# One unit's front split by heads, squares taken in pairs, five transposes moved to DMA

## The chip, the cores and the metric

The kernel runs on one core of one Trainium2 chip. The metric is the device time of one execution in microseconds (us). The profile records one execution and gives its span.

Engine names are those of the profile: PE does the matrix products, PEld its weight loads, DVE is the vector engine, ACT the scalar engine, POOL is GpSimd, and SP shows nothing but issues of DMA in these profiles. "SPq" and "POOLq" mean the issuing of DMA by those engines. Every program here has two DMA queues that matter: q1, fed by SP (`hardware_dynamic` on the page, 72528 packets before), and q0, fed by POOL (`software_dynamic`, 1088 packets).

A run is called fast or slow by comparing its time with the fastest run of the same kernel in the same batch, so a batch in which every run is long is called fast throughout. I therefore also say "short" for runs below 186 us and "long" for runs above 186 us when I speak of the kernel before, whose 47 later runs have nothing between 184.62 and 186.91.

## The reference

A gated linear recurrence over 768 positions, with 4 batches, 8 heads and head size 48, feeds a dense block with squared relu.

```python
def _attn_ref(q, k, v, alpha):
    state = np.zeros((B, H, D, D), dtype=np.float32)
    for t in range(S):
        state = alpha[:, :, t, :, None] * state + np.einsum('bhd,bhe->bhde', k[:, :, t], v[:, :, t])
        y[:, :, t] = np.einsum('bhd,bhde->bhe', q[:, :, t], state)
    return y

def _moe_ref(x, w_in, w_out):          # x: 3072 x 384, w_in: 384 x 2048, w_out: 2048 x 384
    h = x @ w_in
    r = np.maximum(h, 0.0)
    return (r * r) @ w_out
```

## The kernel before

The work is cut into 12 units of 256 tokens (4 batches, 3 stages). Each unit has a *front* (cumulative decay from alpha, scaled k and q, their transposes), the attention products, a transpose of the attention output `xbf` into `xt`, and the dense block: `s1` (w_in), relu, square, `s2` (w_out).

The program is a list of operations. A scheduler written in Python plays it through with estimated costs, and what comes out is a **fixed order of instructions for each engine**. In the traces each engine takes its list in that order and waits on semaphores. So a late input stops what stands behind it in the same list: in the long profile of after ACT was idle for 9.20 us before the cast of a late v (37.91 us), and the four instructions behind it in the list started after it (38.66 to 39.76 us).

The parts that the argument touches:

```python
# all of them move by DMA; order of the loads is steered by "after"
def weight(lay, w):
    cut = slice(w * FS * 128, (w + 1) * FS * 128) if lay == 0 else slice(w * FS, (w + 1) * FS)
    if lay == 0:
        src, dst = moe_w_in.rearrange("(kk p) n -> p kk n", p=128)[:, :, cut], WIN[:, :, cut]
    else:
        src = moe_w_out[w * FS * 128:(w + 1) * FS * 128, :].rearrange("(p e) n -> p (e n)", e=FS)
        dst = WOUT[:, cut, :].rearrange("p e n -> p (e n)")
    key = ("win", "wout")[lay]
    load_op[key, w] = add("pool", lambda e: e.dma_start(dst, src), ...,          # queue q0
                          after=[load_op[AFTER[key, w]]] if (key, w) in AFTER else [])

def load(g):                                                                     # queue q1
    for j, t, nm in ((0, alpha, "a"), (1, k, "k"), (2, q, "q"), (3, v, "v")):
        src = t[b, :, t0:t0 + T, :].rearrange("h (p j) d -> p h (j d)", j=2)     # pieces of 384 bytes
        ...
AFTER = {("win", 0): (1, "a"), ("win", 1): (1, "a"), 2: ("win", 0), ("wout", 0): (2, "a"),
         ("wout", 1): (2, "a"), 3: ("wout", 0)}

# the attention output of a unit, transposed by PE
def xtr(pe):
    for c in range(2):
        for kk in range(KT):
            o = c * KT + kk
            ins = pe.matmul(to[:, c, kk], src[:, o * 128:(o + 1) * 128], IDENT[:], is_transpose=True)
    return ins
add("pe", xtr, ..., reads=[("xbf", x2), ("ident",)], writes=[("ps", "X", 0)])
add("dve", lambda e: e.tensor_copy(dst, bank[:, 0:KT * T]), ..., writes=[("xt", s)])   # or ACT

# relu and square, 512 elements at a time
add("act", lambda e, hb=hb, rb=rb: e.activation(RR[rb][:], psH[hb], AF.Relu), ...)     # or DVE
add("dve", lambda e, dst=dst, sq=sq: e.tensor_tensor(dst, sq, sq, ALU.mult), 415, ...) # or POOL or ACT
# ... (cut)
pr.schedule()
pr.fill(...)       # dummy matmuls ("fillers") in PE's early gaps
pr.place()         # semaphore waits
pr.emit()
```

In words, the start is a chain of loads. Alpha of the second unit lands, then w_in is issued. w_in lands, then alpha, k, q, v of the third unit are issued on q1. When alpha of the third unit lands, w_out is issued on q0. When w_out lands, the loads of the fourth unit are issued. I count units from one; the chain view and the code count them from zero.

## Time and profile before

| | value |
|---|---|
| three timed runs | 191.17, 191.76, 192.35 us |
| the profiled execution | span 180.1 us, time 181.86 us, granted PE clock 1.00 |
| PE, DVE, ACT busy | 174.7, 130.6, 118.6 us |

The profile's page of the kernel before, in part. The second line is busy time with its share of the span and the number of instructions; the row of digits is PE's busy tenths in 40 slices of the span; the queue lines give packets, megabytes and share of the 16 DMA engines.

```profile
span 180.1 us, 5336 instructions
...
PE 174.7 (97%) x2333; PEld 138.7 (77%) x2333; DVE 130.6 (73%) x228; ACT 118.6 (66%) x220; POOL 17.7 (10%) x25
...
PE   7998999999999999999999999999999999999994
...
q1 hardware_dynamic: 72528, 28.32, 65.3%
q0 software_dynamic: 1088, 3.15, 9.2%
```

PE is busy in nearly every slice. q0 carries 1088 packets for 3.15 MB, q1 carries 72528 packets for 28.32 MB: the packets of q0 are large, those of q1 small.

PE's list of waits in the same kernel (engine, line, what it waited for: us in total, times, longest):

```profile
PE psO L896 <- DVE zero L417: 1.3, 1, 1.3
PE psWH L822 <- DMA win<-in_moe_w_in_dram: 0.7, 1, 0.7
PE psWH L541 <- ACT lab L535: 0.4, 1, 0.4
```

The third line: the cumulative-sum product of the third unit waits 0.4 us for an ACT result.

The chain of waits of the same kernel (start us, us, what), only its long DMA pieces:

```profile
4.23 4.86 DMA raw<-in_alpha_dram
...
9.38 8.61 DMA win<-in_moe_w_in_dram
...
18.00 5.32 DMA raw<-in_alpha_dram
...
23.61 8.45 DMA wout<-in_moe_w_out_dram
...
35.72 5.47 DMA raw<-in_v_dram
```

One load releases the next up to about 41 us; after that the chain is nearly all PE work. Two groups of instructions that the change touches (line, engine, operation, count, busy us, mean ns, then idle time before them):

```profile
L836 DVE TENSOR_TENSOR gt<-rr 128x512 bf16<-128x512 bf16 x61 | 26.5, 438 | 19.8 <-ACT rr L830 19.4
...
L774 PE MATMUL psX<-ident,xbf 128*128 128x128 bf16 x72 | 6.0, 219 | 0.1
```

### The profile page before, as it was taken

To read this page: it belongs to the slowest core of one execution; us is meant where nothing else is said; L and a number is where in the kernel's file an instruction comes from. 1 tells how busy PE (TensorE), PEld (TensorE's weight loads), DVE (VectorE), ACT (ScalarE), POOL (GpSimd) and SP (SyncE) were. 2 spreads that over 40 slices of the span, in tenths; PEclk is the share of its full clock that TensorE was granted. 3 is DMA by queue.
4 is the path that set the end of the run, shared out by engine and by line. 5 is a ranking of instruction groups with operands and counts; after the bars stand their busy time and mean duration, and the time that the engine had idled before them with its cause. 6 is when DMAs were issued, how large, how long until landed. Compare 5 with 4: busy or idle time off the path is not lost.

```text
span 180.1 us, 5336 instructions
## 1 busy us (share of the span) xinstructions
PE 174.7 (97%) x2333; PEld 138.7 (77%) x2333; DVE 130.6 (73%) x228; ACT 118.6 (66%) x220; POOL 17.7 (10%) x25
## 2 busy tenths in 40 slices
PE   7998999999999999999999999999999999999994
PEld 5786887866787688877688778787788787788773
DVE  6499577898977988969998888789649655534130
ACT  4762788677786887858677758567557554656451
POOL 3030020323020010242002101000000000000000
DMA  5999999999999998999999994713512510110112
GB/s 147 323 290 192 253 249 207 222 264 284 210 279 235 302 254 221 250 260 279 271 188 306 274 266 136 153 56 60 107 44 34 130 47 0 47 44 0 47 44 87
DMA packets 73639, 31.80 MB, mean 177 GB/s; under 512 B 69392, under 2 KB 72592, under 8 KB 73616
## 3 DMA queue, kind: packets, MB, share of 16 engines
q1 hardware_dynamic: 72528, 28.32, 65.3%
q0 software_dynamic: 1088, 3.15, 9.2%
q8 instruction: 18, 0.29, 0.7%
q14 instruction: 5, 0.04, 0.1%
HBM read 25.17 MB, written 4.72 MB: 166 GB/s over the span
## 4 chain that ended last, share of the span: by engine, by line
PE 74%; DMA 18%; SPq 4%; DVE 2%; issue 1%; ACT 1%
PE psO L853 30%; PE psWH L822 30%; DMA raw<-in_alpha_dram 6%; DMA win<-in_moe_w_in_dram 5%; DMA wout<-in_moe_w_out_dram 5%; SPq L495 4%; DMA raw<-in_v_dram 3%; PE psX L678 3%; PE psX L671 2%; PE psX L732 2%; PE psZ L651 2%; PE psX L774 2%; PE psX L795 1%; PE psZ L732 1%; PE psWH L541 1%
## 5 line engine op out<-in xcount | busy, mean ns | idle before, releaser
L822 PE MATMUL psWH<-xt,win 128*128 128x256 bf16 x576 | 73.3, 274 | 0.9 <-DMA win<-in_moe_w_in_dram 0.7
L822 PEld LDWEIGHTS psWH<-xt,win 128*128 128x128 bf16 x576 | 64.9, 145 | 5.6 <-DVE kqt L622 1.0
L853 PE MATMUL psO<-wout,gt 128*128 128x384 bf16 x368 | 68.9, 326 | 0.1
L830 ACT ACTIVATE rr<-psWH 128x512 bf16<-128x512 f32 x80 | 47.1, 595 | 22.5 <-PE psWH L822 21.2
L853 PEld LDWEIGHTS psO<-wout,gt 128*128 128x128 bf16 x368 | 34.5, 98 | 18.7 <-DMA wout<-in_moe_w_out_dram 0.4
L836 DVE TENSOR_TENSOR gt<-rr 128x512 bf16<-128x512 bf16 x61 | 26.5, 438 | 19.8 <-ACT rr L830 19.4
L839 ACT ACTIVATE gt<-rr 128x512 bf16<-128x512 bf16 x35 | 21.5, 626 | 1.6 <-DVE rr L832 1.2
L860 ACT ACTIVATE osb<-psO 128x384 f32<-128x384 f32 x22 | 10.8, 490 | 13.9 <-PE psO L853 13.6
L741 DVE TENSOR_TENSOR pm<-psX,caus 128x1024 bf16<-128x1024 f32 x12 | 14.7, 1221 | 4.0 <-PE psZ L732 4.0
L741 DVE TENSOR_TENSOR pm<-psZ,caus 128x1024 bf16<-128x1024 f32 x12 | 14.6, 1216 | 0.3 <-PE psZ L732 0.2
L601 DVE TENSOR_TENSOR qks<-raw,ek 128x768 bf16<-128x768 f32 x12 | 12.2, 1019 | 2.9 <-ACT ek L520 2.9
L832 DVE TENSOR_SCALAR rr<-psWH 128x512 bf16<-128x512 f32 x16 | 11.0, 690 | 3.7 <-PE psWH L822 3.6
L896 PE MATMUL psO<-zero 128*128 128x256 bf16 x81 | 12.2, 302 | 1.3 <-DVE zero L417 1.3
L759 ACT ACTIVATE xbf<-psX 128x768 bf16<-128x768 f32 x9 | 7.3, 810 | 8.0 <-PE psZ L651 5.4
L601 DVE TENSOR_TENSOR qks<-raw,eq 128x768 bf16<-128x768 f32 x12 | 11.4, 952 | 0.3 <-POOL eq L569 0.3
L896 PEld LDWEIGHTS psO<-zero 128*128 128x128 bf16 x81 | 8.4, 109 | 2.9 <-DVE zero L417 1.3
L779 DVE COPY xt<-psX 128x768 bf16<-128x768 bf16 x11 | 6.1, 556 | 4.7 <-PE psX L774 4.7
L534 POOL TENSOR_TENSOR prd<-raw 128x384 f32<-128x384 f32 x5 | 5.4, 1084 | 33.7 <-DMA raw<-in_alpha_dram 33.7
L597 POOL CAST vbf<-raw 128x768 bf16<-128x768 f32 x5 | 4.7, 939 | 28.8 <-DMA raw<-in_v_dram 21.1
L678 PE MATMUL psX<-vbf,pm 64*128 64x48 bf16 x384 | 6.9, 180 | 0.0
L598 ACT ACTIVATE vbf<-raw 128x768 bf16<-128x768 f32 x7 | 5.9, 840 | 1.3 <-DMA raw<-in_v_dram 1.3
L704 DVE TENSOR_TENSOR tmp<-psZ,sbd 128x384 f32<-128x384 f32 x8 | 4.4, 550 | 3.0 <-PE psZ L651 3.0
(106 smaller groups left out, 162.2 us busy)
## 6 DMA issues: line engine op xcount, KB each, us to landing
raw<-in_alpha_dram SPq DMA_DIRECT2D x12, 384.0 KB, 4.5
raw<-in_k_dram SPq DMA_DIRECT2D x12, 384.0 KB, 4.8
raw<-in_q_dram SPq DMA_DIRECT2D x12, 384.0 KB, 5.3
raw<-in_v_dram SPq DMA_DIRECT2D x12, 384.0 KB, 5.2
out_dram<-osb SPq DMA_DIRECT2D x23, 192.0 KB, 2.4
win<-in_moe_w_in_dram POOLq DMA_DIRECT2D x2, 768.0 KB, 10.0
wout<-in_moe_w_out_dram POOLq DMA_DIRECT2D x2, 768.0 KB, 10.0
kqt<-qks SPq DMA_TRANSPOSE x18, 4.6
```

The lines of the kernel that those rows point to most:

```text
L601: add("dve", lambda e, a=a, E=E: e.tensor_tensor(QKS[qs][:, a, :, :, 0:D], RAW[r][:, 1 + a].rearrange("p h j d -> p j h d"), E[la][:].rear ...
L678: ins = pe.matmul(psX[:, c, h * D:(h + 1) * D], PM[pm][64 * c:64 * c + 64, n // 2, rr_, n % 2, jk, :], VBF[vb][64 * c:64 * c + 64, h, jk, ...
L741: add("dve", lambda e, hf=hf, psT=psT: e.tensor_tensor(PM[pm][:, hf].rearrange("p r n j t -> p (r n) (j t)"), psT[:, :, :].rearrange("p r ...
L759: add("act", lambda e: e.activation(XBF[x2][:], psX[:, :, 0:HD], AF.Copy), act_ns(2 * HD), p0 + 6100, reads=[("ps", "X", 0), ("ps", "X", 1 ...
L822: ins = pe.matmul(psH[hb][:, i * T:(i + 1) * T], WIN[:, kk, hidden(fj)], XT[s][:, kk].rearrange("p j t -> p (j t)"), start=(kk == 0), stop ...
L830: add("act", lambda e, hb=hb, rb=rb: e.activation(RR[rb][:], psH[hb], AF.Relu), act_ns(512), pu + 600, reads=[("ps", "H", hb)], writes=[(" ...
L832: alts={"dve": (lambda e, hb=hb, rb=rb: e.tensor_scalar(RR[rb][:], psH[hb], 0.0, None, ALU.max), dve_ns(512))})
L836: add("dve", lambda e, dst=dst, sq=sq: e.tensor_tensor(dst, sq, sq, ALU.mult), 415, pu + 1200, reads=[("rr", rb)], writes=[("gt", gt, fj) ...
L839: "act": (lambda e, dst=dst, sq=sq: e.activation(dst, sq, AF.Square), act_ns(512))})
L853: ins = pe.matmul(psS, GT[gt][:, fj, j, :], WOUT[:, fj, :], start=(fj == 0), stop=(fj == FT - 1))
L860: add("act", lambda e, ob=ob, psS=psS: e.activation(OSB[ob][:], psS, AF.Copy), act_ns(DM), ps_ + 700, reads=[keyS], writes=[("osb", ob)], ...
L896: pr.fill(lambda pe: pe.matmul(psO[:, 0:256], ZERO[:, 0:128], ZERO[:, 0:256], skip_group_check=True), 109, min(o.start for o in pr.order[" ...
```

## The change

The intent is threefold. The first unit's front runs in two groups of four heads, so that its first half can start when half of alpha has landed. The squares take two relu results in one instruction, to save time on DVE and ACT. The attention output of the last five units is transposed by DMA instead of PE, to take work off the fullest engine.

The diff, cut to its core (helpers for half keys, the body of `front_by_heads` and pieces that only rename are left out):

```diff
+    PE_X = 7
+    BY_HEADS = (0,)
-    RR = sb("rr", [128, 512], BF16, NRR)
+    RR = sb("rr", [128, 2, 512], BF16, NRR)
 ...
+        for x in range(2) if g in BY_HEADS else ():
+            hs = slice(4 * x, 4 * x + 4)
+            src = alpha[b, hs, t0:t0 + T, :].rearrange("h (p j) d -> p h (j d)", j=2)
+            dst = RAW[r][:, 0, hs].rearrange("p h j d -> p h (j d)")
+            add("sp", lambda e, dst=dst, src=src: e.dma_start(dst, src), 600, L_PRIO[g] + x * 0.5, ...)
 ...
     def front(g):
+        if g in BY_HEADS:
+            front_by_heads(g, p0)
+            return
 ...
+        if g >= PE_X:
+            to = XT[s][:].rearrange("p k j t -> p (k j t)").rearrange("p (a t) -> p a t", t=128)
+            add("sp", lambda e: e.dma_start_transpose(to, src), 1300, p0 + 6700, reads=[("xbf", x2)],
+                writes=[("xt", s)], name=f"xt{g}", dma=f"x{s}", lag=1400)
+            return
 ...
-            hb, rb = h_i[0] % 2, rr_i[0] % NRR
+            hb, rb, half = h_i[0] % 2, h_i[0] // 2 % NRR, h_i[0] % 2
 ...
+            if half == 0 and u < nb - 2:
+                continue
+            k = 2 if half == 1 and u < nb - 2 else 1
+            dst = GT[gt][:, (u + 1 - k) * per:(u + 1) * per].rearrange("p f j t -> p (f j t)")
+            sq = RR[rb][:, half + 1 - k:half + 1].rearrange("p a t -> p (a t)")
```

The scheduler plans the whole program anew after any of these, so the order changes on every engine. With all three parts switched off, the changed source gives exactly the order of before.

More of the change, by code (lines that the diff above doesn't have):

```diff
@@ L45 @@
     SWITCH = 95
+    HALVED = {"qks": 3, "kqt": 3, "raw": 3, "ek": 3, "eq": 3, "acm": 2, "laf": 2}
     AFFINITY = 2500
@@ L58, in add @@
             alts=None):
+        reads, writes = ([h for k in keys for h in ((k + (0,), k + (1,)) if len(k) == self.HALVED.get(k[0]) else (k,))]
+                         for keys in (reads, writes))
         choices = {eng: (fn, cost)}
@@ L351, in bass_gla_recurrent__then__act_relu_squared_kernel @@
     PE_TRANSPOSED = 3
+    PE_X = 7
+    FRONT = {0: 0, 1: 13000, 2: 26000}
+    ATTN = {}
+    DENSE = {}
+    V_CAST = {}
     RATIO = 4
@@ L355, in bass_gla_recurrent__then__act_relu_squared_kernel @@
     TR_RING = "sp"
-    AHEAD = 1
     LATE_STATE = (1, 2)
+    BY_HEADS = (0,)
     BY_TOKEN = (0, 1)
@@ L474, in bass_gla_recurrent__then__act_relu_squared_kernel @@
     load_op = {}
-    SW_LOADS = G
     def hd(ap):
@@ L486, in load @@
         sr, sw = 2 * b + i % 2, 2 * b + (i + 1) % 2
-        ring, cost = ("sp", 600) if g < SW_LOADS else ("pool", 930)
-        for j, t, nm in ((0, alpha, "a"), (1, k, "k"), (2, q, "q"), (3, v, "v")):
+        for x in range(2) if g in BY_HEADS else ():
+            hs = slice(4 * x, 4 * x + 4)
+            src = alpha[b, hs, t0:t0 + T, :].rearrange("h (p j) d -> p h (j d)", j=2)
+            dst = RAW[r][:, 0, hs].rearrange("p h j d -> p h (j d)")
+            add("sp", lambda e, dst=dst, src=src: e.dma_start(dst, src), 600, L_PRIO[g] + x * 0.5,
+                writes=[("raw", r, 0, x)], name=f"lda{x}_{g}", dma=f"a{r}{x}", lag=615)
@@ L490, in load @@
+        for j, t, nm in ((0, alpha, "a"), (1, k, "k"), (2, q, "q"), (3, v, "v"))[g in BY_HEADS:]:
             src = t[b, :, t0:t0 + T, :].rearrange("h (p j) d -> p h (j d)", j=2)
             dst, key = RAW[r][:, j], ("raw", r, j)
-            if nm == "v" and ring == "pool":
-                dst, key = VBF[vb], ("vbf", vb)
-            dst = dst[:].rearrange("p h j d -> p h (j d)")
+            ring, cost, gate = "sp", 600, AFTER.get(g)
+            if nm == "v" and g in V_CAST:
+                dst, key = VBF[vb][:], ("vbf", vb)
+                ring, cost, gate = "pool", 930, V_CAST[g]
+            dst = dst.rearrange("p h j d -> p h (j d)")
@@ L495, in load, with front_by_heads, lanes, m1 @@
             load_op[g, nm] = add(ring, lambda e, dst=dst, src=src: e.dma_start(dst, src), cost, L_PRIO[g] + j,
                 writes=[key], name=f"ld{nm}{g}", dma=f"{nm}{r}{ring}", lag=1230,
-                after=[load_op[AFTER[g]]] if g in AFTER else [])
+                after=[load_op[gate]] if gate else [])
+    def front_by_heads(g, p0):
+        r, la, qs, kt, vb = (g % n for n in (NRAW, 2, NQKS, NKQT, NV))
+        N = HD // 2
+        def lanes(t, x):
+            return t[la][:].rearrange("p j (x n) -> p j x n", x=2)[:, :, x]
+        for x in range(2):
+            hs = slice(4 * x, 4 * x + 4)
+            bank, key = psX[:, x], [("ps", "X", x)]
+            px = p0 + 40 * x
+            add("act", lambda e, hs=hs: e.activation(LAF[la][:, :, hs, 0:D].rearrange("p j h d -> p h j d"),
+                RAW[r][:, 0, hs], AF.Ln), act_ns(HD) + 30, px + 100, reads=[("raw", r, 0, x)], writes=[("laf", la, x)],
+                name=f"ln{x}_{g}")
+            def m1(pe, hs=hs, bank=bank, x=x):
+                mov = [LAF[la][:, j, hs, 0:D] for j in range(2)]
+                pe.matmul(bank[:, 0:N], LINC[:], mov[0], start=True, stop=False, skip_group_check=True)
+                pe.matmul(bank[:, N:HD], LINC[:], mov[0], start=False, stop=False, skip_group_check=True)
+                pe.matmul(bank[:, N:HD], LINC[:], mov[1], start=False, stop=True, skip_group_check=True)
+                pe.matmul(bank[:, 0:N], LSTR[:], mov[1], start=False, stop=True, skip_group_check=True)
+                pe.matmul(bank[:, HD:HD + 4], HSEL[:], HCOL[:, 0:4], start=False, stop=False, skip_group_check=True)
+                for p in range(2):
+                    for j in range(2):
+                        ins = pe.matmul(bank[:, HD + 2 * p:HD + 2 * p + 2],
+                                        LAF[la][:, j, 4 * x + 2 * p:4 * x + 2 * p + 2, :].rearrange("p h d -> p (h d)"),
+                                        ONES2[:], start=False, stop=True, skip_group_check=True)
+                return ins
+            add("pe", m1, pe_ns(4, N) + pe_ns(5, 8), px + 300,
+                reads=[("laf", la, x), ("linc",), ("lstr",), ("ones",), ("hsel",), ("hcol",)], writes=key,
+                name=f"m1{x}_{g}")
+            sums = bank[:, 0:HD].rearrange("p (j n) -> p j n", j=2)
+            add("act", lambda e, x=x, sums=sums: e.activation(lanes(EK, x), sums, AF.Exp, scale=-1.0), act_ns(HD),
+                px + 500, reads=key, writes=[("ek", la, j, x) for j in range(2)], name=f"ei{x}_{g}")
+            add("act", lambda e, x=x, sums=sums: e.activation(lanes(EQ, x), sums, AF.Exp), act_ns(HD),
+                px + 510, reads=key, writes=[("eq", la, j, x) for j in range(2)], name=f"ea{x}_{g}")
+            add("act", lambda e, x=x, bank=bank: e.activation(ACM[la][:, 4 * x:4 * x + 4], bank[:, HD:HD + 4], AF.Exp),
+                act_ns(4), p0 + 560 + x, reads=key, writes=[("acm", la, x)], name=f"ec{x}_{g}")
+        if g not in V_CAST:
+            vin, vout = RAW[r][:, 3].rearrange("p h j d -> p (h j d)"), VBF[vb][:].rearrange("p h j d -> p (h j d)")
+            add("pool", lambda e: e.tensor_copy(vout, vin), 830, p0 + 900, reads=[("raw", r, 3)], writes=[("vbf", vb)],
+                name=f"vc{g}", alts={"act": (lambda e: e.activation(vout, vin, AF.Copy), act_ns(2 * HD))})
+        for x in range(2):
+            hs = slice(4 * x, 4 * x + 4)
+            px = p0 + 40 * x
+            for a, E, nm in ((0, EK, "ek"), (1, EQ, "eq")):
+                add("dve", lambda e, a=a, E=E, hs=hs, x=x: e.tensor_tensor(
+                    QKS[qs][:, a, :, hs, 0:D], RAW[r][:, 1 + a, hs].rearrange("p h j d -> p j h d"),
+                    lanes(E, x).rearrange("p j (h d) -> p j h d", h=4), ALU.mult), dve_ns(HD), px + 1500 + 10 * a,
+                    reads=[("raw", r, 1 + a, x), (nm, la, 0, x), (nm, la, 1, x)], writes=[("qks", qs, a, x)], name=f"{nm}m{x}_{g}")
+            for a in range(2):
+                bank, psk = psZ[:, a, :].bitcast(BF16), [("ps", "Z", a)]
+                def tr(pe, a=a, bank=bank, hs=hs):
+                    for j in range(2):
+                        for n in range(2):
+                            src = QKS[qs][:, a, j, hs].rearrange("p h d -> p (h d)")[:, n * 128:n * 128 + 128]
+                            o = (2 * j + n) * 128
+                            ins = pe.matmul(bank[:, o:o + 128], src, IDENT[:], is_transpose=True)
+                    return ins
+                add("pe", tr, pe_ns(4, 128), px + 2500 + a, reads=[("qks", qs, a, x), ("ident",)], writes=psk,
+                    name=f"tr{a}{x}_{g}")
+                to = KQT[kt][:, a, :, 2 * x:2 * x + 2]
+                at = bank[:, 0:512].rearrange("p (j n s) -> p j n s", j=2, n=2)
+                add("dve", lambda e, to=to, at=at: e.tensor_copy(to, at), dve_ns(512, 2), px + 3000 + a, reads=psk,
+                    writes=[("kqt", kt, a, x)], name=f"et{a}{x}_{g}",
+                    alts={"act": (lambda e, to=to, at=at: e.activation(to, at, AF.Copy), act_ns(512))})
@@ L584, in front @@
         t0 = i * T
-        p0 = (g - AHEAD) * P if g > 2 else g * P
+        p0 = FRONT.get(g, (g - 1) * P)
+        if g in BY_HEADS:
+            front_by_heads(g, p0)
+            return
         r, la, qs, kt, pm, vb, x2 = (g % n for n in (NRAW, 2, NQKS, NKQT, NPM, NV, 2))
@@ L593, in front @@
             decays_by_pair(g, p0, r, la, last)
-        if g < SW_LOADS:
+        if g not in V_CAST:
             vin, vout = RAW[r][:, 3].rearrange("p h j d -> p (h j d)"), VBF[vb][:].rearrange("p h j d -> p (h j d)")
@@ L690, in state @@
         b, i, sr, sw = names(g)
-        p0 = g * P
+        p0 = ATTN.get(g, g * P)
         la, x2 = g % 2, g % 2
@@ L717, in scores, with tiles, run @@
     def scores(g):
-        p0 = g * P
+        p0 = ATTN.get(g, g * P)
         kt, pm = g % NKQT, g % NPM
         halves = ((psX, "X"), (psZ, "Z"))
-        def run(pe):
-            for hf, (psT, key) in enumerate(halves):
-                for nn in range(2):
-                    for jk in range(2):
-                        for c in range(2):
-                            for rr_ in range(2):
-                                n = 2 * hf + nn
-                                o = (nn * 2 + jk) * 128
-                                d0 = 64 * rr_
-                                ins = pe.matmul(psT[64 * c:64 * c + 64, rr_, o:o + 128],
-                                                KQT[kt][d0:d0 + 64, 0, jk, n, 64 * c:64 * c + 64],
-                                                KQT[kt][d0:d0 + 64, 1, :, n, 64 * c:64 * c + 64])
-            return ins
-        add("pe", run, pe_ns(32, 128, 4), p0 + 3800, reads=[("kqt", kt, 0), ("kqt", kt, 1)],
-            writes=[("ps", key, c) for _, key in halves for c in range(2)], name=f"p{g}", mode=("T", "T"))
+        def tiles(hfs):
+            def run(pe):
+                for hf in hfs:
+                    psT = halves[hf][0]
+                    for nn in range(2):
+                        for jk in range(2):
+                            for c in range(2):
+                                for rr_ in range(2):
+                                    n = 2 * hf + nn
+                                    o = (nn * 2 + jk) * 128
+                                    d0 = 64 * rr_
+                                    ins = pe.matmul(psT[64 * c:64 * c + 64, rr_, o:o + 128],
+                                                    KQT[kt][d0:d0 + 64, 0, jk, n, 64 * c:64 * c + 64],
+                                                    KQT[kt][d0:d0 + 64, 1, :, n, 64 * c:64 * c + 64])
+                return ins
+            return run
+        for hfs in ((0,), (1,)) if g in BY_HEADS else ((0, 1),):
+            add("pe", tiles(hfs), pe_ns(16 * len(hfs), 128, 4), p0 + 3800 + hfs[0],
+                reads=[("kqt", kt, a, hf) for a in range(2) for hf in hfs],
+                writes=[("ps", halves[hf][1], c) for hf in hfs for c in range(2)], name=f"p{hfs[0]}_{g}",
+                mode=("T", "T"))
         for at, hf in enumerate((1, 0) if g in LATE_STATE else (0, 1)):
@@ L747, in output @@
     def output(g, with_state):
-        p0 = g * P
+        p0 = ATTN.get(g, g * P)
         x2 = g % 2
@@ L781, in output @@
             alts={"act": (lambda e: e.activation(dst, bank[:, 0:KT * T], AF.Copy), act_ns(KT * T))})
-    rr_i = [0]
     h_i = [0]
@@ L809, in moe @@
         per = 512 // T
-        p0 = g * P + 20500
+        p0 = DENSE.get(g, g * P + 20500)
         nb = FT // per
         for u in range(nb):
-            hb, rb = h_i[0] % 2, rr_i[0] % NRR
+            hb, rb, half = h_i[0] % 2, h_i[0] // 2 % NRR, h_i[0] % 2
             h_i[0] += 1
-            rr_i[0] += 1
             pu = p0 + u * P * 0.5 / nb
@@ L821, in s1 @@
                     for kk in range(KT):
-                        ins = pe.matmul(psH[hb][:, i * T:(i + 1) * T], WIN[:, kk, hidden(fj)],
-                                        XT[s][:, kk].rearrange("p j t -> p (j t)"),
+                        mov = XT[s][:, kk].rearrange("p j t -> p (j t)")
+                        if g >= PE_X:
+                            mov = XT[s][:].rearrange("p k j t -> p (k j t)").rearrange(
+                                "p (c k j t) -> p k j c t", c=2, k=KT, j=2)[:, kk]
+                        ins = pe.matmul(psH[hb][:, i * T:(i + 1) * T], WIN[:, kk, hidden(fj)], mov,
                                         start=(kk == 0), stop=(kk == KT - 1))
@@ L829, in moe @@
                 writes=[("ps", "H", hb)], name=f"s1_{g}_{u}")
-            add("act", lambda e, hb=hb, rb=rb: e.activation(RR[rb][:], psH[hb], AF.Relu), act_ns(512), pu + 600,
-                reads=[("ps", "H", hb)], writes=[("rr", rb)], name=f"re{g}_{u}",
-                alts={"dve": (lambda e, hb=hb, rb=rb: e.tensor_scalar(RR[rb][:], psH[hb], 0.0, None, ALU.max),
+            rr = RR[rb][:, half]
+            add("act", lambda e, hb=hb, rr=rr: e.activation(rr, psH[hb], AF.Relu), act_ns(512), pu + 600,
+                reads=[("ps", "H", hb)], writes=[("rr", rb, half)], name=f"re{g}_{u}",
+                alts={"dve": (lambda e, hb=hb, rr=rr: e.tensor_scalar(rr, psH[hb], 0.0, None, ALU.max),
                               dve_ns(512))})
-            dst = GT[gt][:, u * per:(u + 1) * per].rearrange("p f j t -> p (f j t)")
-            sq = RR[rb][:]
-            add("dve", lambda e, dst=dst, sq=sq: e.tensor_tensor(dst, sq, sq, ALU.mult), 415, pu + 1200,
-                reads=[("rr", rb)], writes=[("gt", gt, fj) for fj in fjs], name=f"sq{g}_{u}",
-                alts={"pool": (lambda e, dst=dst, sq=sq: e.tensor_tensor(dst, sq, sq, ALU.mult), 1040),
-                      "act": (lambda e, dst=dst, sq=sq: e.activation(dst, sq, AF.Square), act_ns(512))})
+            if half == 0 and u < nb - 2:
[3 more added lines that the diff above has]
+            sq = RR[rb][:, half + 1 - k:half + 1].rearrange("p a t -> p (a t)")
+            add("dve", lambda e, dst=dst, sq=sq: e.tensor_tensor(dst, sq, sq, ALU.mult), 148 + k * 267, pu + 1200,
+                reads=[("rr", rb, h) for h in range(half + 1 - k, half + 1)],
+                writes=[("gt", gt, fj) for fj in range((u + 1 - k) * per, (u + 1) * per)], name=f"sq{g}_{u}",
+                alts={"pool": (lambda e, dst=dst, sq=sq: e.tensor_tensor(dst, sq, sq, ALU.mult), 200 + k * 840),
+                      "act": (lambda e, dst=dst, sq=sq: e.activation(dst, sq, AF.Square), act_ns(k * 512))})
         for j in range(2):
```

## The prediction

> What bounds the kernel now. The page's busy table gives the matmul engine (PE) 174.7 us of 180.1 (97%); DVE 73%, ACT 66%. The chain of waits has DMA pieces up to 42.1 us (alpha load to 9.1, w_in to 18.0, alpha of the third unit to 23.3, w_out to 32.1, v of the fourth unit to 41.2) and practically only PE pieces from 42.2 to 177.6. PE's own list of waits is 2.8 us, 1.3 of them before its first instruction. So from 18.1 us, when the first w_in matmul starts (w_in landed at 18.0, its activations at 17.3), PE is a full queue; its only slack is ten filler matmuls (about 1.1 us) and some 0.6 us of waiting.
>
> What the change does.
> 1. Squares of two relus. DVE's square of 128x512 takes 0.43 us; from the 0.55 and 0.95 us of products of 384 and 768 elements I estimate 0.15 us fixed cost per instruction, so a pair costs about 0.69 us. Three pairs per unit, 36 in all, save about 5 us of DVE and ACT time. Those engines are not the bottleneck: worth 0 to 0.3 us.
> 2. First unit in two halves. Attention output y0 should start some 2 us earlier than 14.4 us. But the first w_in matmul still waits for w_in, which is issued when the second unit's alpha lands. That depends on bytes moved (each 393 KB load took about 1.15 us at the DMA's rate in the issue list), and the bytes are the same, so w_in lands at 18.0 +- 0.3 us. The earlier front becomes idle or filler time. In the built order ten fillers still stand behind the first w_in matmul, as before. Worth -0.3 to +0.5 us.
> 3. DMA transposes for the last five units. Each removes six PE transposes, 0.33 to 0.34 us in the chain of waits [...], and an eviction of 0.56 us on DVE or 0.8 us on ACT. PE saves 5 x 0.335 = 1.7 us, all in the PE-only part of the chain. Latency: the existing transposes of 128x8x128 land 3.1 to 6.2 us (median 3.4) after issue in the second half, where the DMA share falls from 0.73 to 0.14. With 0.8 us for the copy to xbf and the hops the input is ready 4.5 to 7 us after the attention matmuls. The built order puts 6.8 to 8.5 us of other PE work between (my sum of traced durations), so it should be hidden; the unit right after the last loads is the tightest. The w_in matmuls now read runs of 64 elements; the cumulative-sum matmuls already read runs of 48 and are spaced 0.16 us for 384 columns, [...]so no loss.
>
> Sum: 1.7 us from transposes, about 0.2 from the rest: span 178.2 us, time 189.9 us. Range 188.5 to 191.3. Chances: faster by over 2% 0.06, within 2% 0.92, slower 0.02.
>
> What would show it. Groups: the PE transposes of xbf fall from 12 to 7 groups and the w_in matmul keeps its 0.109 us spacing. Chain: the first w_in matmul still starts at 17.8 to 18.4 us, released by w_in, with a longer PE gap or more waiting before it. PE's list of waits: under 0.3 us for xt. DVE and ACT together some 8 us less busy, PE's share unchanged at about 97%.
>
> What would make it wrong. A transpose delayed in the in-order SP queue behind a store or behind loads leaves PE waiting for xt [...]. The static order built for shorter or longer waits than the chip's leaves gaps between 18 and 42 us. Or the earlier front does shift the load chain: then up to 2 us more.

## The result, and the profile after

A ratio below is the mean time of one kernel's fast runs over the mean of the other's fast runs in the same rounds, so it is not quite the ratio of the medians that I quote.

The first comparison gave, for the changed kernel, 192.74, 191.14, 185.53 and 184.69 us (median 188.33), and for the kernel before 191.17 to 192.35 (four runs, median 191.70). Ratio of fast runs: 0.9655, interval 0.9592 to 0.9718. The median lies a little below the predicted range, but the spread is the news: the four runs of the changed kernel are in two groups 7 us apart, and its two fast runs were compared with four runs of before that were all long. The profiled execution of before (181.86 us) is shorter than the shortest run of after.

The profiled execution after is the long one of 192.74 us. Its page in part, with PEclk the granted PE clock in tenths:

```profile
span 191.0 us, 5241 instructions
...
PE 175.8 (92%) x2301; PEld 138.6 (73%) x2301; DVE 123.1 (64%) x199; ACT 119.6 (63%) x214; POOL 19.3 (10%) x27
...
PE   7998895069999999999999999999999999999994
...
PEclk9999999558999999999999999999999999999999
...
q1 hardware_dynamic: 76544, 29.30, 65.3%
q0 software_dynamic: 1088, 3.15, 8.7%
```

The seventh and eighth slice (one slice is 4.8 us) hold a hole in PE, and the clock is at half in the eighth and ninth. Everywhere else PE is as full as before. The list of waits names it (L629 answers to L541 of before, L928 to L822):

```profile
PE psWH L629 <- ACT acm L646: 8.9, 1, 8.9
PE psO L1007 <- DVE zero L426: 1.3, 1, 1.3
PE psWH L928 <- DMA win<-in_moe_w_in_dram: 1.2, 1, 1.2
```

PE waits once, for 8.9 us, on an ACT result. The chain of waits tells why ACT was late:

```profile
4.79 5.68 DMA raw<-in_alpha_dram
...
10.76 8.73 DMA win<-in_moe_w_in_dram
...
23.88 14.00 DMA raw<-in_v_dram
37.91 0.84 ACT vbf L689
38.75 0.39 ACT ek L641
39.16 0.50 ACT eq L643
39.68 0.19 ACT acm L646
39.92 0.50 PE psWH L629
```

v of the third unit needs 14.00 us from issue to landing; the median of all twelve v loads in that profile is 5.2 us. ACT stands at the cast of that v (`vbf`), and the work that PE needs stands behind the cast in ACT's list. The trace shows it: ACT is idle for 9.20 us until v has landed, and the pieces then follow the cast without a gap, 37.91 to 39.87 us.

The groups that the change touches, after (the first two answer to L836 of before and to its squares on ACT, the last to L774: 42 transposes are left of 72; "+1 forms" says that the mean mixes 128x1024 with 128x512):

```profile
L946 DVE TENSOR_TENSOR gt<-rr 128x1024 bf16<-128x1024 bf16 (+1 forms) x44 | 26.0, 596 | 28.9 <-ACT rr L936 28.6
...
L950 ACT ACTIVATE gt<-rr 128x1024 bf16<-128x1024 bf16 (+1 forms) x16 | 13.9, 869 | 1.6 <-DVE rr L938 1.3
...
L871 PE MATMUL psX<-ident,xbf 128*128 128x128 bf16 x42 | 3.5, 219 | 0.1
```

With the shapes kept apart, a pair of 1024 elements on DVE takes 0.70 us where two single ones take 0.87 us. DVE is 7.5 us less busy than before, ACT about the same.

### The profile page after: what moved, and what is told of

Read it like the earlier page. It is cut to its first block, busy times and chain, and to the rows that moved or that the text cites. A ratio compares the mean times of both kernels' runs of the same rounds, so it can differ in the third digit from the quotient of the medians.

```text
span 191.0 us, 5241 instructions
## 1 busy us (share of the span) xinstructions
PE 175.8 (92%) x2301; PEld 138.6 (73%) x2301; DVE 123.1 (64%) x199; ACT 119.6 (63%) x214; POOL 19.3 (10%) x27
## 3 DMA queue, kind: packets, MB, share of 16 engines
q0 software_dynamic: 1088, 3.15, 8.7%
## 4 chain that ended last, share of the span: by engine, by line
PE 75%; DMA 15%; SPq 4%; ACT 4%; issue 1%
PE psO L964 31%; PE psWH L928 30%; DMA raw<-in_v_dram 7%; DMA win<-in_moe_w_in_dram 5%; SPq L510 4%; DMA raw<-in_alpha_dram 3%; PE psX L769 3%; PE psX L762 2%; PE psX L825 2%; PE psZ L742 2%; PE psX L898 1%; ACT vbf L689 1%; PE psZ L825 1%; PE psWH L629 1%; PE psX L871 1%; ACT eq L643 1%
## 5 line engine op out<-in xcount | busy, mean ns | idle before, releaser
L928 PE MATMUL psWH<-xt,win 128*128 128x256 bf16 x576 | 74.6, 278 | 1.3 <-DMA win<-in_moe_w_in_dram 1.2
L928 PEld LDWEIGHTS psWH<-xt,win 128*128 128x128 bf16 x576 | 65.5, 145 | 6.6 <-issue 1.4
L936 ACT ACTIVATE rr<-psWH 128x512 bf16<-128x512 f32 x85 | 50.5, 597 | 23.5 <-PE psWH L928 21.9
L946 DVE TENSOR_TENSOR gt<-rr 128x1024 bf16<-128x1024 bf16 (+1 forms) x44 | 26.0, 596 | 28.9 <-ACT rr L936 28.6
L971 ACT ACTIVATE osb<-psO 128x384 f32<-128x384 f32 x22 | 10.8, 491 | 11.7 <-PE psO L964 11.3
L950 ACT ACTIVATE gt<-rr 128x1024 bf16<-128x1024 bf16 (+1 forms) x16 | 13.9, 869 | 1.6 <-DVE rr L938 1.3
L622 POOL TENSOR_TENSOR prd<-raw 128x384 f32<-128x384 f32 x7 | 7.8, 1121 | 62.3 <-DMA raw<-in_alpha_dram 62.3
L689 ACT ACTIVATE vbf<-raw 128x768 bf16<-128x768 f32 x8 | 6.7, 841 | 11.3 <-DMA raw<-in_v_dram 11.3
L650 DVE TENSOR_TENSOR ek<-ek,raw 128x384 f32<-128x384 f32 x9 | 5.4, 600 | 10.2 <-ACT ek L641 10.2
L692 DVE TENSOR_TENSOR qks<-raw,ek 128x768 bf16<-128x768 f32 x11 | 10.4, 949 | 0.0
L938 DVE TENSOR_SCALAR rr<-psWH 128x512 bf16<-128x512 f32 x11 | 7.5, 686 | 4.0 <-PE psWH L928 3.9
L629 PE MATMUL psWH<-lab,lstr 128*128 128x384 bf16 x2 | 0.8, 413 | 8.9 <-ACT acm L646 8.9
```

The costliest lines, as they stand in the source:

```text
L689: name=f"vc{g}", alts={"act": (lambda e: e.activation(vout, vin, AF.Copy), act_ns(2 * HD))})
L692: add("dve", lambda e, a=a, E=E: e.tensor_tensor(QKS[qs][:, a, :, :, 0:D], RAW[r][:, 1 + a].rearrange("p h j d -> p j h d"), E[la][:].rear ...
L928: ins = pe.matmul(psH[hb][:, i * T:(i + 1) * T], WIN[:, kk, hidden(fj)], mov, start=(kk == 0), stop=(kk == KT - 1))
L936: add("act", lambda e, hb=hb, rr=rr: e.activation(rr, psH[hb], AF.Relu), act_ns(512), pu + 600, reads=[("ps", "H", hb)], writes=[("rr", rb ...
L950: "act": (lambda e, dst=dst, sq=sq: e.activation(dst, sq, AF.Square), act_ns(k * 512))})
L971: add("act", lambda e, ob=ob, psS=psS: e.activation(OSB[ob][:], psS, AF.Copy), act_ns(DM), ps_ + 700, reads=[keyS], writes=[("osb", ob)], ...
```

## The theories

**Theory A, a race of two queues, in both kernels.** w_out is issued on q0 when alpha of the third unit lands. k, q and v of the third unit are then still in flight on q1. The theory is that a DMA engine which still holds packets of v when the packets of w_out reach it takes the two in turn. A packet of w_out (6144 bytes) takes about 0.48 us in the records, a packet of v (384 bytes) 0.022 to 0.035 us, so the last few packets of v on that engine would take many times as long. v then lands late (14.00 us after its issue in the long profile of after), the cast on ACT waits for it (9.20 us), PE waits for ACT (8.9 us), and PE's clock is 0.50 from 34.4 to 44.6 us. The kernel before has the same loads, hence it has a long state too; the timed runs were in it and the profile was not.

**Rival B.** The long state is a state of the chip (a lower clock over the whole run) and has nothing to do with the order of the loads.

**Rival C.** The change itself, its earlier front or its DMA transposes, makes v late, and before's 191 us is something else.

The expectations below use the letters more freely: "theory B" in e1 to e4 is that the change saves work, or that a later w_out only costs time; "rival C" in e5 is that the DMA engines are slow for a while whatever the size of the packets; A2 and B2 in e8 are about the halved front alone.

The packet records of the long profile of after fit A. From 30 to 35 us of the profile 10 to 14 small packets of q1 start in each microsecond, beside 32 to 44 of w_out, and 44 of these 56 lie in series of three or more in which the next one starts 0.485 to 0.488 us after the last, about one packet of w_out (median 0.474 us) later. That the packets of a series share one DMA engine is an estimate from this spacing, since the records used do not tell the engines apart. More on this under e13.

## The experiments

Each call ran its kernels and the kernel before on one chip: e1 to e4 on a first, e5 to e8 on a second, e9 to e12 on a third, e13 to e16 on a fourth. All results were correct. The edits, used in several runs:

```diff
 # "gate": w_out is issued only when q (or v) of the third unit has landed; no instruction changes its place
+    for w in range(WS):
+        load_op["wout", w].deps[load_op[2, "q"]] = True      # e2, e6, e8;  e3 has "v"
     pr.place()

 # "small packets": rows of w_out padded, so that a DMA piece is one row of 768 bytes, not 8 rows of 6144 bytes
-    WOUT = nc.alloc_sbuf_tensor("wout", [128, FT, DM], BF16)
+    WOUT = nc.alloc_sbuf_tensor("wout", [128, FT, DM + 16], BF16)
-    ....rearrange("(p e) n -> p (e n)", e=FS);  dst = WOUT[:, cut, :].rearrange("p e n -> p (e n)")
+    ....rearrange("(p e) n -> p e n", e=FS);    dst = WOUT[:, cut, 0:DM]
-    WOUT[:, fj, :]
+    WOUT[:, fj, 0:DM]

 # parts of the change alone, from the changed source
-    BY_HEADS = (0,)          # no halved front
+    BY_HEADS = ()
-    PE_X = 7                 # no DMA transposes
+    PE_X = 12
-    half = h_i[0] % 2, ...   # no pairs
+    half = 0; k = 1
```

Neither the gate nor the padding changes the order of instructions on any engine, which was compared list by list (in the traces too every engine's list is the same, instruction for instruction). The padding does also make w_out's tile larger, and POOL takes 0.9 instead of 0.6 us to issue each half of w_out; the gate, which changes neither, is the check on that.

### e1: the changed kernel again

No edit.

> The changed kernel once more, to see its states. Theory A (a race of two DMA queues): w_out is issued when the third unit's alpha lands; if any DMA engine then still holds packets of that unit's v load, the 0.4 KB packets of v take turns with the 6 KB packets of w_out and v lands up to 14 us after its issue instead of about 5.5, ACT and then PE stand still for about 9 us and the granted clock falls. Then the times fall in two groups: near 185 us at clock 1.00 and near 191 to 193 us at clock 0.97 to 0.98. Theory B (the change saves work, the long runs of the changed kernel are an outside disturbance): nearly all runs near 185 us, and the unchanged kernel stays at 191.7 in all of them with clock 1.00.

Measured: 182.44, 184.35, 186.34, 187.75, 190.13 and 193.52 us, median 187.05; before in the same rounds 181.93 to 191.86, median 190.75, with four of its eleven runs at 181.9 to 182.6. Fast to fast the ratio is 1.0061 (0.9967 to 1.0155). So both kernels have short and long runs, and like for like no gain shows. The two groups that theory A expected are not there, though: the six runs of the changed kernel are spread over the whole of 182 to 194 us. The profiled run was of middle length, 187.75 us, and its stall is of middle length too:

```profile
PE psWH L629 <- ACT acm L646: 4.5, 1, 4.5
PE psWH L928 <- DMA win<-in_moe_w_in_dram: 1.5, 1, 1.5
```

There v landed 10.15 us after its issue. Times of 187.75 and 192.74 us with stalls of 4.5 and 8.9 us: 5.0 us of time for 4.4 us of stall. B, which has no stall in it, does not predict this.

### e2 and e3: before, w_out issued later

> The kernel before, every engine's instruction order unchanged, only that w_out's issue also waits for the third unit's q (which lands about 2.4 us after its alpha). Theory A: most of v's packets are drained when w_out starts, so the wait for v is gone in most executions: 181 to 186 us against 191.7. Theory B: w_out only comes 2 to 3 us later, so the time stays at 191.7 or rises by up to 3 us.

> As e2, but w_out waits for the third unit's v itself, so the two transfers cannot overlap at all. Theory A: no execution has a long v load; w_out lands some 4 us later than in the profile of before, which costs PE up to 3 us of waiting for w_out: 182 to 187 us, all runs within 1%, clock 1.00. Theory B: 193 to 196 us.

Measured: e2 182.62 to 184.92 us (median 183.87), no long run in six; ratio to before's fast runs 1.0077 (1.0020 to 1.0134). e3 184.32 to 188.59 (median 185.74), ratio 1.0173 (1.0126 to 1.0219). In the same rounds seven of eleven runs of before were above 188 us. The later w_out removes the state at 191 us. What it costs is that PE then waits for w_out, 2.7 us in e3; in e2 it is 0.9 us, with 1.4 us for a relu and 1.0 us for the cumulative-sum product beside it. The expectation for e3 (all runs within 1%, clock 1.00) was missed: the runs are 2.3% apart, and five of six have a clock of 0.991. In the profiled one of these the clock fell to half for 3.41 us behind the wait. The run at 188.59 us was not traced, so what made it longer is not known.

### e4: the DMA transposes alone

> The kernel before plus the DMA transposes of the last five units alone (front and squares as before; with all three parts off this source gives the instruction order of before exactly). Instruction order of the first 100 us is that of before, so theory A expects the state of before: nearly all runs in the long group, 191.7 minus 1.7 = 190 us. Theory B, if the transposes are the main part of the gain: 185 to 188 us. In both, PE waits under 0.3 us for the transposed tiles.

Measured: 192.14, 190.19, 190.91, 191.10, 181.77 and 180.94 us, median 190.55; ratio of the fast runs 0.9950 (0.9901 to 0.9998) on two fast runs. The order is then that of before (in the traces every engine's list is the same up to 110 us, where PE's first transpose is missing), and the long state is there all the same, so the halved front is not its cause. In the profiled long run v landed 12.91 us after its issue and PE waited 7.7 us behind it.

### e5: before with small packets

> The kernel before with w_out stored in rows of 400 elements of which 384 are used, so that its DMA moves 128x8x384 pieces (0.8 KB written each) where it moved 128x3072 (6 KB); same instruction order, same waits, same start. Theory A [...]: v packets left over when w_out starts now wait behind 0.8 KB packets, so v is at most some 2 us late, the group at 188 to 192 us disappears: all runs 181.5 to 185 us at clock 0.99 to 1.00. Rival C (in some executions the DMA engines are simply slow for a while, and w_out only happens to be there): packet size does not matter, and two thirds of the runs stay at 188 to 192 us, as the 11 of 15 runs of before so far.

Measured: 182.38 to 185.16 us (median 182.59), no long run in six; before in the same rounds had five of eleven at 190.19 to 192.37. Ratio to before's fast runs 1.0020 (0.9966 to 1.0074). The profile has 2880 packets on q0 where before has 1088, and a packet of w_out takes 0.08 us instead of 0.48. w_out is issued at 23.66 us, as early as before (23.61), and lands after 8.39 us (8.45).

This is the test of the mechanism: same order, same issue time, same bytes, only the size of the pieces (and the padding), and the long state is gone. Rival C of the expectation, slow engines whatever the packet size, would have left some four long runs in six.

### e6, e7, e8: parts of the change, w_out gated

> The changed kernel, instruction order unchanged, with w_out's issue also waiting for the third unit's q, to be set against e2 (183.9 us), which is the same edit on the kernel before. If the change saves PE work as predicted (1.7 us from the transposes, 0.2 from the rest) this gives 182.0 us. From the fast executions so far (changed 182.4 to 185.5, before 181.9 to 182.6) I rather expect 183.5 to 185.5 us, so no gain at equal state. In both cases no run above 187 us.

> placeholder look: the DMA transposes alone again, one profile, to see a fast or a long execution of it: 181 to 182 us or 190 to 192 us, nothing between.

> The front of the first unit in two groups alone, with w_out waiting for q, to be set against e2 (183.9 us). In both profiles of the changed kernel the second unit's alpha landed 0.6 to 1.1 us later than in the profiles of before (10.2 and 10.7 against 9.4 to 9.9), and everything to w_out hangs on it. Theory A2 (the extra issue of the split alpha load delays the load chain): 184.3 to 185.3 us. Theory B2 (the front only gives slack): 183.5 to 184.2 us.

Measured: e6, the whole change with w_out after q, 182.28 to 184.42 us, median 183.03, ratio 1.0048 (0.9995 to 1.0100), no long run. The label of e7 misleads: by my mistake the kernel that ran was the transposes alone *without* the gate. It took 190.73 us, with v landing 13.13 us after its issue and PE waiting 8.5 us, as e4. e8, the halved front alone and gated, took 185.86 to 188.88 us, median 186.37, ratio 1.0208 (1.0169 to 1.0247). That is above both expectations (at most 185.3 us), and it holds the cost of the gate too (1.0077 in e2, on another chip), so e12 below is the cleaner figure for the halved front.

### e9 to e12: the change and its parts, with small packets

> The changed kernel with the w_out transfer in 0.8 KB pieces (the edit of e5), order and waits unchanged: the value of the whole change with the stall taken out, to be set against e5 (182.6 us). If my blind sum holds, 180.7 us; if the fast executions seen so far tell it (changed 182.4 to 185.5 against 181.6 to 182.9), 182.5 to 184.5 us. No run over 187 us in either case.

> The transposes alone, w_out in 0.8 KB pieces. Blind sum: five times 0.335 us less PE work gives 182.6 - 1.7 = 180.9 us. From the fast executions of e4 (180.9 and 181.8) 181 to 181.7 us. This should be the fastest version, under both kernels.

> The squares of two relus alone, w_out in 0.8 KB pieces, against e5 (182.6). Blind: minus 0 to 0.3 us. Rival: the second half of each pair has to wait, so the order leaves PE gaps while 18 to 42 us (the built order has 86 fillers against 81): plus 0.5 to 2 us.

> The front of the first unit in two groups alone, w_out in 0.8 KB pieces, against e5 (182.6). Blind: 0 with an error of 0.5 us. From e8 (186.4 against 183.9 for the same edit without it, on another chip) plus 1.5 to 2.5 us, with the second unit's alpha landing 0.5 us or more later than the 9.4 us of before and the rest in waits of PE between 18 and 45 us.

| run | what is in it | median us | ratio to before's fast runs | interval |
|---|---|---|---|---|
| e9 | all three parts | 182.86 | 1.0051 | 0.9969 to 1.0133 |
| e10 | DMA transposes alone | 182.48 | 1.0012 | 0.9958 to 1.0066 |
| e11 | pairs of squares alone | 183.86 | 1.0083 | 1.0020 to 1.0146 |
| e12 | halved front alone | 185.81 | 1.0202 | 1.0140 to 1.0264 |

In the same rounds before ran from 180.96 to 192.04 us (median 185.20). No run of these four kernels has the stall's 188 us and more, also in e12, whose own level is 185 to 187.

Against e5's 182.59 us, e9 came out as the fast runs had suggested and not as the blind sum. e10, expected at 180.9 to 181.7 us, missed. e11 is 1.3 us longer, as its rival said. e12 is 3.2 us longer, more than the 1.5 to 2.5 us expected.

The parts do not add up: +0.8% and +2.0% alone, but +0.5% together with the transposes. Each part makes the scheduler plan anew. In e12 PE is 16.42 us busy of the 18 us from 42 to 60 us (17.75 in e14, the order of before), with waits of 0.4 and 0.9 us there:

```profile
43.59 1.48 PE L961 MATMUL psO<-wout,gt 128*128 128x384 bf16 x8 [0.42 <-ACT osb L968]
...
49.14 1.53 PE L928 MATMUL psWH<-xt,win 128*128 128x256 bf16 x12 [0.90 <-ACT xt L885]
```

These are lines of e12's timeline (start us, us, group, idle before it and what ended that). From the first w_out product to the last group of PE it is 145.7 us in e12 and 142.8 in e14, so most of what the halved front costs alone is lost there. That these are gaps of the new plan rather than of the part itself, and that the plan is the reason of the non-additive sum, is an argument; I did not run a kernel with the order held fixed.

### e13: before again, one look

No edit. Until here the one profile of the unaltered kernel before had been of a short execution.

> The unchanged kernel before, one profiled look, to catch its long state directly. Queue-race theory: if the execution is above 188 us, v of the third unit lands 10 us or more after its issue instead of 5.5, the cast of v on ACT ends late, and PE has one idle stretch of 4 to 9 us between 28 and 42 us, as in the long profile of the kernel after; the rest of the kernel is as in the fast profile, within 1 us. If it is below 185 us, v lands within 7 us and PE waits under 3.5 us in all. Rival (the long state of the kernel before is something else, a lower clock spread over the whole run): a long execution has no such stretch.

Measured: 190.64 us, clock 0.982; a long execution. PE's waits:

```profile
PE psWH L541 <- ACT lab L535: 6.6, 1, 6.6
PE psO L896 <- DVE zero L417: 1.3, 1, 1.3
PE psWH L822 <- DMA win<-in_moe_w_in_dram: 1.2, 1, 1.2
```

Its chain of waits:

```profile
4.24 5.37 DMA raw<-in_alpha_dram
...
9.90 9.06 DMA win<-in_moe_w_in_dram
...
22.80 11.88 DMA raw<-in_v_dram
34.71 0.84 ACT vbf L598
35.55 0.42 ACT lab L535
36.02 0.50 PE psWH L541
```

And three stretches of it (from:to, length, then busy us and instructions of PE, PEld, DVE, ACT, POOL, the PE clock, the DMA share, GB/s):

```profile
29.00:36.00 7.00, 0.44 (x5) 0.16 (x2) 1.73 (x4) 1.29 (x3) 0.00 (x0) 0.81 1.02 219
36.00:38.00 2.00, 1.98 (x14) 1.50 (x15) 0.56 (x1) 1.64 (x4) 0.00 (x0) 0.50 0.97 250
...
41.00:42.00 1.00, 1.00 (x9) 0.61 (x8) 0.76 (x2) 0.61 (x2) 1.00 (x2) 1.00 0.00 1
```

The same wait that took 0.4 us in the short execution took 6.6 us here, for the same reason as after: v late (11.88 us), cast late, PE late. The DMA engines were busy all the time and moved as much (219 GB/s from 29 to 36 us, 217 GB/s in the short execution); it is the order of packets, not their amount, that differs.

The 8.8 us of span between the two executions of the one kernel can be laid out. The w_in products start 0.98 us later (w_in landed at 18.96 instead of 17.99). The first cumulative-sum product of the third unit starts 7.15 us later (36.02 against 28.87), 6.2 of which is the longer wait. The first w_out product starts 8.49 us later (40.60 against 32.11): 1.3 us were added after the stall, where the clock is at half. From there to the start of the last group the two take 143.0 and 142.7 us. B is out: nothing after 41 us is slower. So is C: this is the kernel before.

On the clock, e13 shows this: PE idles from 29.4 us, the clock is 0.50 from 33.3 to 40.1 us (6.83 us), and PE is busy again from 36.0 us. Twelve w_in products took 2.76 us there, and 1.53 us before the stall. In e3 PE was idle for 2.73 us, and the clock was 0.50 for 3.41 us after it.

The packet records of three executions, counted for each microsecond (queue q1 means the small packets of k, q, v and alpha; q0 the packets of w_out; the microseconds of these records run about 0.8 us ahead of the profile's):

```
us of the records      26   27   28   29   30   31   32   33   34   35   36
before, short    q1   667  101    0    0    0    0    0    0  300  652  637
                 q0     8   30   33   34   47   38   36   34   25    2    1
before, long e13 q1   499  608   76    6    6    7    8    6   10  401  692
                 q0     0   10   33   32   35   45   35   36   33   24    5
small packets e14 q1  669   81    0    0    0    0    0    0   59  645  847
                 q0    17  195  229  257  266  270  269  264  245   63    5
```

In the short execution the last packets of the third unit's loads, of which v is the last, are through just as w_out arrives. In the long one some 43 of them trickle through over six microseconds beside w_out. An estimate from these numbers: 34 large packets a microsecond over the 16 DMA engines that the profile's page counts are about two for each engine, so 6 to 10 small ones a microsecond are three to five engines that alternate one for one, each with some 12 to 14 packets left. The start times of the small packets point to three: 38 of the 43 lie in series in which the next one starts 0.486 us (to 3 ns) after the last, about one large packet (0.474 us) later, with three such series side by side. With small packets there is no tail that lasts.

What decides whether v is through in time may be a margin of tenths of a microsecond: w_out is issued 1.74 us after v in the short execution (23.61 and 21.87 us) and 1.43 to 1.54 us after it in the five profiles with a late v (after, e1, e4, e7 and e13). In e5 and e14 it is 1.43 and 1.44 us, as little as in the long ones, and with the small packets no v took more than 6.7 us to land. With one short profile of large packets the margin is a hint and no proof; what moves it from run to run stays open.

### e14, e15, e16: without the long state, on one chip

e14 is e5's kernel, e15 e10's, e16 e9's.

> The same kernel as e5 (w_out in 768-byte pieces), here on the same chip as e15 and e16, so that these three can be compared without the chip's own part. Expected: median 182.3 to 183.0 us, no run above 186.

> Same as e10 (DMA transposes of the last five units alone, w_out in small packets). If the 1.6 us that PE saves after the first w_out matmul come through, 1.0 to 1.7 us below e14. If they are given back at the start (the first w_out matmul comes about 1.3 us later, because w_out lands later), within 0.4 us of e14. Between e5 and e10, on different chips, the difference was 0.1 us, so I expect the second.

> Same as e9 (the whole change, w_out in small packets). If the halved front costs the 0.5 us that its load chain comes later and the transposes bring 1.6, then 0 to 1.1 us below e14, that is 181.5 to 182.7 us. If the front and the squares cost more than the transposes bring, as the heads alone (+2 per cent) and the pair alone (+0.8 per cent) would add up to, above e14 by 3 us or more. I expect within 0.6 us of e14.

| run | what is in it | runs us | median us | ratio to before's fast runs | interval |
|---|---|---|---|---|---|
| e14 | none of the change | 181.82 to 184.73 | 182.65 | 1.0001 | 0.9950 to 1.0053 |
| e15 | DMA transposes alone | 181.16 to 183.31 | 181.89 | 0.9981 | 0.9920 to 1.0042 |
| e16 | the whole change | 181.62 to 183.74 | 182.45 | 1.0026 | 0.9961 to 1.0091 |

Before in the same rounds: six runs of 181.31 to 183.37 us, six of 191.09 to 192.33, median 187.23. Differences of medians between the three: -0.76 us for the transposes, -0.20 us for the whole change. No two of them are told apart by the intervals. e14 and e16 came as expected; e15 lies between its two expectations (1.0 to 1.7 us below e14, or within 0.4).

The timelines show where the transposes' gain is and where it goes. The first w_out product and the start of the last group of PE:

| | first w_out product | last group | between |
|---|---|---|---|
| before, short | 32.11 | 174.83 | 142.7 |
| e5, e14 | 32.10, 32.04 | 175.34, 174.80 | 143.2, 142.8 |
| e10, e15 (transposes) | 33.42, 33.07 | 175.07, 175.01 | 141.7, 141.9 |
| e9, e16 (all) | 33.23, 32.49 | 174.80, 174.56 | 141.6, 142.1 |

Between the two points the kernels with transposes are 0.7 to 1.7 us shorter than e5 and e14, about 1.2 us on average: PE does less. But they reach the first w_out product later, by 1.0 to 1.3 us with the transposes alone and by 0.4 to 1.1 with the whole change. In e15 PE waits there first for v's chain and then for w_out, whose landing sets the start (lines of e14's timeline, then of e15's):

```profile
32.04 1.48 PE L853 MATMUL psO<-wout,gt 128*128 128x384 bf16 x8 [0.70 <-DMA wout<-in_moe_w_out_dram]
```

```profile
29.39 0.34 PE L629 MATMUL psWH<-lab,linc 128*128 128x384 bf16 x1 [1.28 <-ACT lab L623]
...
33.07 1.47 PE L961 MATMUL psO<-wout,gt 128*128 128x384 bf16 x8 [0.56 <-DMA wout<-in_moe_w_out_dram]
```

w_out landed 9.34 us after its issue in e15, 9.24 in e10, against 8.47 and 8.39 without the transposes; in e9 and e16, which are the same kernel, it was 9.15 and 7.54. I could not settle why. The transposes' plan is not the reason: in e10 and e15 every engine's list is that of before up to 110 us, long after this point. Over the 14 profiles in which w_out is not gated its landing takes 7.52 to 9.34 us, a wider spread than the gain, so the later start in e10 and e15 is not shown to be a cost of the transposes.

For the whole change the chain of waits of e16 shows the load chain that the halved front moved:

```profile
5.04 4.82 DMA raw<-in_alpha_dram
...
10.15 8.09 DMA win<-in_moe_w_in_dram
...
18.26 6.01 DMA raw<-in_alpha_dram
...
24.55 7.54 DMA wout<-in_moe_w_out_dram
```

Alpha of the second unit is now the sixth DMA issued instead of the fifth. Its flight takes 4.82 us, as in e14, but it starts at 5.04 instead of 4.29 us, and w_in is issued at 10.15 instead of 9.41 us.

## Why the prediction was wrong, and where it was right

**The step that failed: "So from 18.1 us ... PE is a full queue; its only slack is ten filler matmuls (about 1.1 us) and some 0.6 us of waiting."** That holds for the profiled execution. The prediction then took its sum, "span 178.2 us, time 189.9 us", by adding to the span the 11.7 us by which the timed runs exceeded it, as if that were a constant. The runs show in its place: time minus span is 1.7 to 1.8 us, and the other 9 to 10 us are a stall (6.6 us in e13, 8.9 us in the long run of after), a slow clock behind it (about 1.3 us) and a later start (1.0 us). They come in some executions and not in others: 25 of 47 later runs of before are long (186.91 to 192.37), 22 are short (180.96 to 184.62). A median of such a mixture is a matter of how many of each kind were drawn, so 191.7 against 188.3 said nothing on the change, and 0.9655 is a ratio across states.

**"PE saves 5 x 0.335 = 1.7 us, all in the PE-only part of the chain."** The mechanism is right. The transposes are off PE (42 are left of 72), and no wait for `xt` shows in the second half: in e10 they land 2.7 to 3.2 us after issue. The size was somewhat high: 0.7 to 1.7 us, about 1.2, between the first w_out product and the last group. It did not reach the end of these profiles, since they come to the first w_out product 0.4 to 1.3 us later; for the transposes alone this is not due to the plan, which is before's up to 110 us, but to a later landing of w_out whose cause is open. Nor do the times settle it: 0.9950 (e4), 1.0012 (e10) and 0.9981 (e15), with intervals of half a per cent and more to each side, leave room for no gain and for 1.2 us. The prediction's check in the list of waits (under 0.3 us for xt) held. Six transposes take 0.33 to 0.36 us in the chains, 55 to 60 ns each; the prediction took 0.335.

**"So w_in lands at 18.0 +- 0.3 us", worth "-0.3 to +0.5 us".** Right in e16 (18.24 us), missed in e9 (18.48) and e12 (19.10); but the range was too narrow in any case, since without the halved front it landed at 17.63 to 19.32 us in eleven profiles. What the split does change is the issue: it adds a DMA ahead of the second unit's alpha, so the chain comes later: w_in is issued at 10.14 (e9), 10.15 (e16) and 10.71 us (e12), against 9.38 (before), 9.41 (e14) and 9.68 (e5). Over all profiles it is 9.87 to 10.76 us in the seven with the halved front and 9.29 to 9.91 in the eleven without, 0.7 us later on average. I had counted bytes and not issues; on one chip the chain came 0.74 (e16 and e14), 0.41 (e9 and e10) and 1.20 us later (e12 and e11). Alone, the halved front costs 2% (e12, 1.0202; the 1.0208 of e8 includes the gate), of which the later chain is only a part.

**Squares "worth 0 to 0.3 us".** The estimate of 0.69 us for a pair was right (0.70 us), and DVE is 6 to 7 us less busy with the pairs alone (123.7 us in e11, 129.6 to 131.1 in the profiles with before's order), though a part of that is other work that the new plan gave to POOL (25.4 us busy in e11, 18.3 in e14). Its worth to the time was not: alone the pairs cost 0.8% (e11, 1.0020 to 1.0146). How much of that is theirs is open: w_out landed late in e11's profile too (9.22 us after its issue), and from the first w_out product to the last group it takes 143.8 us against 142.8 in e14.

**"DVE and ACT together some 8 us less busy, PE's share unchanged at about 97%."** Compared with like (e16 and e14): DVE 6.1 us less, ACT 0.2 us more, so 5.9 us together instead of 8, PE at 96%. The lost 97% in the profile after was the stall.

**What would make it wrong: "The static order built for shorter or longer waits than the chip's leaves gaps between 18 and 42 us".** The place was named, the cause not. The stall is in before's order as well, and in no estimate that the order was built on.

In short: the change alone is worth nothing that these runs can tell from zero, 1.0061 (0.9967 to 1.0155) with the race and 1.0026 (0.9961 to 1.0091) without it. What does pay is to take away the race: with w_out in rows of 768 bytes, 36 runs of e5, e9, e10, e14, e15 and e16 all stayed within 181.16 to 185.16 us, so that the medians, 181.89 to 182.86, are below those of both unaltered kernels (before 184.62 to 190.75 in four batches, after 187.05 in e1). Against before's short runs small packets gain nothing (1.0020 in e5, 1.0001 in e14): only the long runs are gone. The best median is e15's, but nothing sets it apart from e14's or from before's short runs.

## What to carry to other kernels

Compare the profiled execution's time with the timed runs before building on the profile; if they differ by more than the fixed part (1.7 to 1.8 us here), first find the other state, and do not call the difference overhead. Here a load that ACT waited for was in flight on one DMA queue when large packets (6144 bytes) were started on another, and it took 10.15 to 14.00 us to land in five profiles, against a median of 5.2 us; with packets of 768 bytes none of 36 runs was long. So look for one load whose landing takes twice its median, and try smaller packets before moving the load. And when a static order is planned anew, expect the gain of a part to be mixed with gaps of the new plan; and before a later start is put down to the new order, check that the order up to there has changed at all.
